# Holding the first superblock's transposing load until W0 has landed

## The chip, the cores and the metric

The kernel runs on one core of a Trainium2 chip. The metric is the device time of one execution in microseconds (us), lower is better. It is measured by repeated executions; beside it stands one execution recorded by the hardware profiler, from which all durations below are taken.

## The reference

A deep-and-cross network with six layers over a batch of 4096 rows with 416 features, all bf16:

```python
B, F, D, L = 4096, 26, 16, 6
Din = min(F * D, 1024)          # 416
def reference(x0, ws, bs):      # x0 [4096,416], ws [6,416,416], bs [6,416]
    x = x0
    for l in range(ws.shape[0]):
        x = x0 * (x @ ws[l] + bs[l]) + x
    return x
```

The kernel carries it as a sum of matrix products that stays in PSUM: each layer adds its product to the running sum, and one VectorE operation per tile adds a bias and multiplies by x0 to make the next layer's input.

## The kernel before

**Tiling.** The batch is cut into NS = 4 superblocks of SB = 1024 rows, and each goes through the L = 6 layers. The 416 features are three blocks of 128 (index c or k, NC = 3) and a tail of 32. Activations are held transposed, with features on partitions: x0T_sb is x0 for the three blocks, x0t_sb the tail. Each superblock has two halves of H = 512 columns. `n = s * L + l` counts the layer steps.

**One layer step on TensorE**, in program order: (1) nine groups of four matmuls, 512 columns each, for half 0 (lines 347 to 363); (2) the tail rows, ten matmuls with 32 rows (lines 388 to 409), which end by adding one to `s_ti`; (3) the tail's own output, twelve matmuls of 256 columns over all 1024 columns (lines 413 to 419); (4) nine groups of four for half 1 (line 420). TensorE runs its instructions in order, so a wait in front of (3) holds everything behind it. VectorE makes the six 128x512 tiles of the next layer (line 527): three for half 0 after (2), three for half 1 as (4) brings them.

**Where the first superblock gets x0T.** Rows 0 to 767 are loaded in natural layout as three 208 KB pieces (`xin_sb`, lines 135 to 137), transposed on TensorE and copied out by VectorE and ScalarE. Rows 768 to 1023 come by a single DMA that transposes on its way, line 157: 256 rows by 384 columns of two bytes, 192 KB. Its semaphore is `s_x0T[0]`. The only instruction that waits for it is TensorE's at line 412, between (2) and (3) of step n = 0, since (3) is the first to read columns 768 to 1023.

**Who issues what at the start.** Before the block: SP issues the biases, `xin_sb` rows 0 to 255 and rows 512 to 767; ScalarE's queue issues `xin_sb` rows 256 to 511, then W0 (`s_w[0]`, 312 KB), then `xtl_sb` (the tail of rows 768 to 1023), then two tail-weight loads; GpSimd issues six small weight loads. In the block SP issues in this order: the transposing load of line 157; W1 (line 163); four tail-weight loads for layers 1 to 5 (line 166, made at line 125, `s_wt[1]`); W2, after the wait at line 160 for `s_ti` to reach 1; and so on. SP runs in order too: a wait on SP stands in front of all of this.

**Who waits for W0.** TensorE at line 346, in front of its first matmul with weights. That matmul also waits, at line 339, for the third VectorE copy of x0T.

**Who waits for the rest of SP's list.** Line 360 waits for W1 ahead of step n = 1, line 378 for `s_wt[1]` ahead of that step's tail rows.

Of the kernel before, what the change touches and what calls it, by code (L numbers as in the profile page):

```python
# [11 lines left out]
def bass_standalone__dcn_v2_cross__recsys_kernel(  # L12
# [20 lines left out]
    with ExitStack() as es:  # L33
# [30 lines left out]
        def sem(name):  # L64
            return es.enter_context(nc.semaphore(name))
# [6 lines left out]
        s_w = [sem("s_w%d" % i) for i in range(L)]  # L72
# [18 lines left out]
        def wmain(l):  # L91
            return ws[l, 0:DF, :].rearrange("(k p) n -> p k n", p=128)
# [12 lines left out]
        def lane(g):  # L105
            return slice(32 * g, 32 * g + 32)
# [9 lines left out]
        def store(eng, a, n, by_pool):  # L116
            eng.wait_ge(s_o, a + n - by_pool)
            if by_pool:
                eng.wait_ge(s_oP, by_pool)
            assert a % 2 == 0 and n == 2  # L120
            eng.dma_start(out_w[:, (j0 + a) // 2, :, :], o_sb[:, j0 + a:j0 + a + n, :]).then_inc(s_out, 16)

        def load_wt(eng, g, a, b, done):
            n0, n1 = ((0, 256), (256, DF))[g % 2]
            eng.dma_start(
                wt_sb[lane(g), a:b, 0:n1 - n0], ws[a:b, DF:D, n0:n1].rearrange("l p n -> p l n")
            ).then_inc(done, 16)
# [19 lines left out]
        @block.sync  # L147
        def _(sp):
            def load_rows(s):
                sp.dma_start_transpose(  # L150
                    x4_sb[:, s - 1:s, :], x0[s * SB:(s + 1) * SB, D - 128:D]
                ).then_inc(s_x4[s - 1], 16)
                sp.dma_start_transpose(
                    x0T_sb[:, :, s * SB:(s + 1) * SB], x0[s * SB:(s + 1) * SB, 0:DF]
                ).then_inc(s_x0T[s], 16)

            sp.dma_start_transpose(x0T_sb[:, :, 768:SB], x0[768:SB, 0:DF]).then_inc(s_x0T[0], 16)
            for l in range(1, L):
                if l > 1:
                    sp.wait_ge(s_ti, (1, 2, 2, 2)[l - 2])  # L160
                if l == L - 1:
                    load_rows(1)
                sp.dma_start(w_sb[:, l, :, :], wmain(l)).then_inc(s_w[l], 16)
                if l == 1:
                    for g in range(4):
                        load_wt(sp, g, 1, L, s_wt[1])
            for s in range(NS - 1):
                n = (s + 1) * L
                sp.wait_ge(s_xa, NC * n)
                sp.wait_ge(s_xb, NC * n)  # L170
                for c in range(NC):
                    sp.dma_start_transpose(
                        o_sb[:, s * JS:(s + 1) * JS, c * 128:(c + 1) * 128], xo_sb[:, s, c, :]
                    ).then_inc(s_oT, 16)
                sp.wait_ge(s_xt, n)
                sp.dma_start_transpose(ot_sb[:, s, :, :], xot_sb[:, s, :]).then_inc(s_ot, 16)
                if s < NS - 2:
                    load_rows(s + 2)
                if s == 0:
                    for g in range(4):  # L180
                        sp.dma_start(wl_sb[lane(g), :], ws[L - 1, DF:D, :]).then_inc(s_wl, 16)
                if s == 1:
                    sp.dma_start(x0n_sb[:, :, :].rearrange("p (g r) d -> p g r d", r=2), x0_w[:, j0 // 2:, :, :]).then_inc(s_x0n, 16)
                sp.wait_ge(s_oT, 16 * NC * (s + 1))
                sp.wait_ge(s_otc, s + 1)
                sp.dma_start(
                    out_v[:, s * JS:(s + 1) * JS, :], o_sb[:, s * JS:(s + 1) * JS, :]
                ).then_inc(s_out, 16)
            store(sp, 0, 2, 0)
            store(sp, 4, 2, 2)  # L190
# [458 lines left out]
```

## Time and profile before

| what | value |
|---|---|
| median of 4 runs | 128.25 us (128.12 to 128.37) |
| the profiled execution, its own time | 128.29 us |
| its span in the profile | 127.0 us |
| TensorE clock granted, every slice | 1.0 in nearly every stretch (9 tenths or more in all 40 slices) |
| DVE busy | 99.9 us (79%) |
| ACT busy | 67.6 us (53%) |
| POOL busy | 24.0 us (19%) |
| mean DMA traffic | 106 GB/s |

The span runs from the first to the last recorded instruction; 1.3 us of the execution's own time lie outside it. PE is TensorE's matmul side and PEld its weight loads, which overlap the matmuls; DVE is VectorE, ACT ScalarE, POOL GpSimd, and a q behind an engine's name means its sequencer, which issues DMAs. Busy shares are averages over the span. Matmul ends are modelled, so a busy PE does not mean that no matmul could have started earlier; where TensorE waited is better read from the starts of its weight loads. Besides the page, the trace holds a start and a size for each DMA packet and the time of each landing (the increment of a semaphore by one of the 16 DMA engines); where a time below has three decimals, it is from these records.

### The profile page before, as it was taken

The page shows a single profiled execution, that of the slowest core. Times are in us where ns is not written, and L with a number is a line of the kernel's source. Part 1 is how long each engine was busy: PE and PEld are TensorE (multiplying, and loading weights), DVE is VectorE, ACT ScalarE, POOL GpSimd, SP SyncE. Part 2 cuts the span into 40 slices and gives each one's busy share as a digit, 9 for nine tenths or more (in the row PEclk, how much of TensorE's full clock was granted, in tenths as well). Part 3 has the DMA queues.
Part 4 walks back from the last instruction along what each step waited for, and adds up shares of the span by engine and source line. Part 5 has one row for each costly group of instructions (what it writes and reads, how often), then busy time and mean ns, then how long its engine had stood idle before and what let it go on. Part 6 is the DMA issues. An engine that isn't in the chain of part 4 may idle for free.

```text
span 127.0 us, 5318 instructions
## 1 busy us (share of the span) xinstructions
PE 123.5 (97%) x2410; PEld 62.4 (49%) x2410; DVE 99.9 (79%) x154; ACT 67.6 (53%) x146; POOL 24.0 (19%) x44
## 2 busy tenths in 40 slices
PE   7999999999999999999999999999999999999991
PEld 5654544444445445445445445445444444454660
DVE  2449779779779779789788797797797797797973
ACT  0637357377726455575744563575762574566830
POOL 7512202102102013022022023022021021220450
PEclk9999999999999999999999999999999999999999
DMA  3963299400009969810007779940005900430006
GB/s 108 316 154 106 81 270 181 110 0 0 5 3 113 168 108 238 260 32 5 5 0 137 137 131 240 355 151 0 5 0 48 210 21 0 164 109 5 0 30 243
DMA packets 32577, 13.49 MB, mean 106 GB/s; under 512 B 24870, under 2 KB 32556, under 8 KB 32556
## 3 DMA queue, kind: packets, MB, share of 16 engines
q1 hardware_dynamic: 31036, 12.12, 43.7%
q10 hardware_dynamic: 1328, 0.99, 2.5%
q8 instruction: 19, 0.31, 1.0%
q0 software_dynamic: 192, 0.06, 0.2%
q14 instruction: 2, 0.02, 0.0%
HBM read 3.86 MB, written 3.41 MB: 57 GB/s over the span
## 4 chain that ended last, share of the span: by engine, by line
PE 97%; DVE 0%; issue 0%
PE ps L255 82%; PE ps L383 10%; PE ps L130 2%; PE ps L439 2%; PE ps L302 1%; PE ps L454 1%; DVE o_sb L540 0%; PE ps L478 0%; PE ps L399 0%; PE ps L484 0%
## 5 line engine op out<-in xcount | busy, mean ns | idle before, releaser
L527 DVE SCALAR_TENSOR_TENSOR xT_sb<-ps,cb_sb,x0T_sb 128x512 bf16<-128x512 f32 x120 | 81.0, 745 | 16.3 <-PE ps L383 16.3
L255 PE MATMUL ps<-xT_sb,w_sb 128*32 128x512 bf16 (+1 forms) x1596 | 84.2, 364 | 0.0
L255 PEld LDWEIGHTS ps<-xT_sb,w_sb 128*32 128x32 bf16 x1596 | 40.9, 97 | 37.2 <-issue 4.0
L556 ACT ACTIVATE xt_sb<-xt_sb 32x256 bf16<-32x256 bf16 x76 | 31.5, 414 | 15.7 <-POOL xt_sb L232 15.1
L585 ACT ACTIVATE t_sb<-ps,cb_sb 64x256 f32<-64x256 f32 x46 | 21.6, 469 | 31.1 <-PE ps L255 30.8
L232 POOL TENSOR_TENSOR xt_sb<-t_sb,x0t_sb 128x256 bf16<-128x256 f32 x20 | 13.4, 672 | 81.4 <-ACT t_sb L585 81.4
L255 PE MATMUL ps<-x0T_sb,w_sb 128*32 128x512 bf16 (+1 forms) x336 | 18.7, 367 | 0.0
L527 DVE SCALAR_TENSOR_TENSOR xo_sb<-ps,cb_sb,x0T_sb 128x512 bf16<-128x512 f32 x18 | 12.1, 744 | 2.5 <-PE ps L383 2.5
L255 PEld LDWEIGHTS ps<-x0T_sb,w_sb 128*32 128x32 bf16 x336 | 8.6, 97 | 7.8 <-issue 1.1
L383 PE MATMUL ps<-xt_sb,wt_sb 32*128 32x512 bf16 x76 | 11.5, 379 | 0.0
L604 ACT ACTIVATE x0t_sb<-x_sb 32x512 bf16<-32x512 bf16 x12 | 7.5, 626 | 0.3
L399 PE MATMUL ps<-xt_sb,wt_sb 32*128 32x512 bf16 x38 | 7.4, 385 | 0.0
L383 PE MATMUL ps<-xt_sb,wc_sb 32*128 32x256 bf16 x76 | 7.3, 268 | 0.0
L383 PEld LDWEIGHTS ps<-xt_sb,wt_sb 32*128 32x128 bf16 x76 | 2.2, 92 | 8.1 <-DVE xT_sb L527 8.1
L383 PEld LDWEIGHTS ps<-xt_sb,wc_sb 32*128 32x128 bf16 x76 | 3.8, 93 | 2.2
L232 POOL TENSOR_TENSOR xot_sb<-t_sb,x0t_sb 128x256 bf16<-128x256 f32 x3 | 2.0, 673 | 12.6 <-ACT t_sb L585 12.6
L540 DVE SCALAR_TENSOR_TENSOR o_sb<-ps,x0n_sb 128x416 bf16<-128x416 f32 x6 | 3.3, 586 | 1.0 <-PE ps L484 0.9
L560 ACT ACTIVATE xo_sb<-ps,cq_sb 128x512 bf16<-128x512 f32 x5 | 3.3, 685 | 1.1 <-PE ps L383 1.1
L551 ACT ACT_TABLE_LOAD x1 | 1.3, 1283 | 3.6 <-issue 3.6
L130 PE MATMUL ps<-const-bfloat16-1.0 128*32 128x256 bf16 x40 | 2.3, 418 | 0.8 <-PEq L634 0.8
L439 PE MATMUL ps<-w_sb,xT_sb 128*128 128x416 bf16 x12 | 2.8, 340 | 0.0
L255 PE MATMUL ps<-w_sb,xT_sb 128*32 128x416 bf16 x48 | 2.6, 339 | 0.0
(52 smaller groups left out, 39.8 us busy)
## 6 DMA issues: line engine op xcount, KB each, us to landing
out_dram<-o_sb SPq DMA_DIRECT2D x3, 832.0 KB, 4.5
w_sb<-in_ws_dram SPq DMA_DIRECT2D x5, 312.0 KB, 3.7
x0n_sb<-in_x_dram SPq DMA_DIRECT2D x1, 832.0 KB, 5.5
xin_sb<-in_x_dram SPq DMA_DIRECT2D x2, 208.0 KB, 3.5
out_dram<-o_sb SPq DMA_DIRECT2D x2, 208.0 KB, 1.9
out_dram<-o_sb ACTq DMA_DIRECT2D x2, 208.0 KB, 2.0
w_sb<-in_ws_dram ACTq DMA_DIRECT2D x1, 312.0 KB, 3.7
xin_sb<-in_x_dram ACTq DMA_DIRECT2D x1, 208.0 KB, 2.6
```

The source lines that it names most:

```text
L130: nc.tensor.matmul(ps[lane(q % 4), 7, 0:256], lhsT=CONST[:, 0:32], rhs=CONST, start=True, stop=True, skip_group_check=True, tile_position= ...
L232: pool.tensor_tensor(out=dst, in0=t32_sb[:, n % 2, :], in1=x0t_sb[:, s, 0:G], op=ALU.mult).then_inc(s_xt, 1)
L255: return pe.matmul(dst, lhsT=lhsT, rhs=rhs, start=start, stop=True, skip_group_check=True, tile_position=(0, 32 * q),)
L383: return pe.matmul(dst, lhsT=lhsT, rhs=srct[lane(g), cols], start=l == 0 and start, stop=True, skip_group_check=True, tile_position=(32 * ...
L399: pe.matmul(ps[:, NC * h + 2, :], lhsT=wt_sb[lane(g), l, 0:128], rhs=srct[lane(g), :].rearrange("p (b r) -> p b r", b=2)[:, ::-1, :], star ...
L439: pe.matmul(ps[:, NAT_BANKS[t], 0:D], lhsT=xT_sb[:, (L - 1) % 2, k, rows], rhs=w_sb[:, L - 1, k, :], start=False, stop=True, skip_group_ch ...
L527: dve.scalar_tensor_tensor(out=dst, in0=ps[:, NC * half + c, :], scalar=cb_sb[:, c, l:l + 1], in1=x0T_sb[:, c, o:o + H], op0=ALU.add, op1= ...
L540: dve.scalar_tensor_tensor(out=o_sb[:, j0 + t, :], in0=ps[:, NAT_BANKS[t], 0:D], scalar=1.0, in1=x0n_sb[:, t, :], op0=ALU.add, op1=ALU.mul ...
L556: ins = act.activation(out=buf[lane(g), G:2 * G], in_=buf[lane(g ^ 1), 0:G], func=ACTF.Copy)
L560: act.activation(out=xo_sb[:, NS - 1, c, half * H:(half + 1) * H], in_=ps[:, NC * half + c, :], func=ACTF.Identity, bias=cq_sb[:, c:c + 1] ...
L585: ins = act.activation(out=t32_sb[HALVES[h], n % 2, :], in_=tail(h), func=ACTF.Identity, bias=cb_sb[HALVES[h], NC, l:l + 1],)
L604: ins = act.activation(out=x0t_sb[lane(g), s + 1, :].rearrange("p (b n) -> p b n", b=2), in_=src[:, ::-1, :] if g % 2 else src, func=ACTF. ...
```

## The change

One wait is added on SP in front of the transposing load of line 157. It waits until W0's semaphore has its full count of 16. Nothing else differs: the load, its semaphore, its reader and the order of SP's list are the same.

```diff
                     x0T_sb[:, :, s * SB:(s + 1) * SB], x0[s * SB:(s + 1) * SB, 0:DF]
                 ).then_inc(s_x0T[s], 16)
 
+            sp.wait_ge(s_w[0], 16)
             sp.dma_start_transpose(x0T_sb[:, :, 768:SB], x0[768:SB, 0:DF]).then_inc(s_x0T[0], 16)
             for l in range(1, L):
                 if l > 1:
```

## The prediction

> **What bounds the kernel.** I read the page first: the busy shares and the chain of work that ended last.
>
> ```profile
> PE 123.5 (97%) x2410; PEld 62.4 (49%) x2410; DVE 99.9 (79%) x154; ACT 67.6 (53%) x146; POOL 24.0 (19%) x44
> ...
> PE 97%; DVE 0%; issue 0%
> ```
>
> TensorE carries the whole chain. Then the table of waits, for TensorE's weight-load side, where its waiting shows (total us, times, longest):
>
> ```profile
> PEld ps L383 <- DVE xT_sb L527: 8.1, 19, 0.4
> ...
> PEld ps L255 <- DMA w_sb<-in_ws_dram: 0.3, 1, 0.3
> ```
>
> Only one DMA ever makes TensorE wait: W0, 0.3 us, once. Now SP's own list and TensorE's weight loads, both in order of time (start, length, what):
>
> ```profile
> 2.22 1.28 SPq L157 DMA_TRANSPOSE x0T_sb<-in_x_dram  x1
> 3.55 0.58 SPq L163 DMA_DIRECT2D w_sb<-in_ws_dram  x1
> 4.17 1.92 SPq L125 DMA_DIRECT2D wt_sb<-in_ws_dram  x4
> 8.74 5.80 SPq L163 DMA_DIRECT2D w_sb<-in_ws_dram  x3
> ```
>
> ```profile
> 8.29 0.11 PEld L383 LDWEIGHTS ps<-x0t_sb,wc_sb 32*128 32x128 bf16 x3
> 8.61 1.96 PEld L255 LDWEIGHTS ps<-x0T_sb,w_sb 128*32 128x32 bf16 x48 [0.21 <-issue]
> 10.68 1.83 PEld L255 LDWEIGHTS ps<-xT_sb,w_sb 128*32 128x32 bf16 x36
> 12.94 0.09 PEld L383 LDWEIGHTS ps<-xt_sb,wt_sb 32*128 32x128 bf16 x1 [0.42 <-DVE xT_sb L527]
> ```
>
> The line at 8.61 is the first reader of the moved load (the matmuls behind line 412). Its 0.21 us of idle is "issue", so it did not wait for the load. The load was issued at 2.22 and took 5.0 us to land, so at 7.24. How late may it be? W0's last landing was 5.014 and the first weight load behind it started at 5.11: 0.10 us from landing to weight load. So the **deadline** is 8.61 - 0.10 = 8.51, and the slack today 8.51 - 7.24 = 1.27 us.
>
> **The change, step by step.**
>
> *SP's wait.* W0's last landing is 5.014. SP answers fast (its W2 issue at 8.736 came 0.02 us after the `s_ti` signal at 8.719), so the load is issued at **5.03** and not 2.22: 2.81 us later, against 1.27 us of slack. If the 5.0 us from issue to landing held, it would land at 10.03 and cost 1.5 us. It will not: in the packet records its 768 packets of 256 bytes start at 4.957, 2.73 us after the issue, because the same queue still carried `xin_sb` until about 5.0. After the change that queue is empty.
>
> *From issue to landing on an empty queue.* The nearest row is the other transposing load from DRAM, 1024 packets (line 150), issued at 43.57. Traffic by stretch (last two columns: DMA share, GB/s):
>
> ```profile
> 44.50:44.75 0.25, 0.25 (x12) 0.11 (x4) 0.25 (x1) 0.00 (x0) 0.25 (x1) 1.00 0.00 0
> 44.75:45.00 0.25, 0.25 (x10) 0.11 (x5) 0.25 (x2) 0.00 (x0) 0.23 (x1) 1.00 0.29 16
> ...
> 46.00:46.50 0.50, 0.50 (x16) 0.21 (x8) 0.50 (x2) 0.49 (x2) 0.00 (x0) 1.00 0.96 205
> 46.50:47.00 0.50, 0.50 (x12) 0.11 (x4) 0.40 (x1) 0.20 (x1) 0.00 (x0) 1.00 0.03 6
> ```
>
> Nothing moves until 44.75; the first packet is at 44.932, 1.36 us after the issue. From the first packet on I use the moved load itself: 4.957 to the landing at 7.238 is 2.28 us (1.2 us of packets, 1.1 us until the last landing, with W1's packets close behind it on the queue, as they will be again). Sum: 5.03 + 1.36 + 2.28 = **8.67**, which is 0.16 us past the deadline. The ends: the fastest transpose on an empty queue (line 172, issued at 66.457, on-chip source) landed after 3.2 us, so 8.23 and no wait; the line 150 loads on an empty queue took 3.4 and 3.5 us with a third more packets; the slow line 176 ones 3.8 and 3.9 us, so 8.93 and 0.42 us. I take 8.67, as it is made from the load's own packets.
>
> Here a rule speaks. The Trainium skill, "Advanced Engine Details and Errata", section "X-Bar Transpose (TRN2)", holds transposing DMAs to be as fast as regular ones. The regular row is W2, 312 KB on an empty queue at 8.74: it landed in 2.95 us. By the rule 192 KB would be there by 5.03 + 2.95 = 7.98, and the change would cost nothing. The transposing rows need 3.4 us for 256 KB where the plain one needs 2.95 for 312 KB, so I go with them.
>
> *What a wait there costs.* The wait stands in front of TensorE's parts (3) and (4). From 8.61 matmul groups follow each other every 0.216 us until 12.84; at 12.94 the tail rows start, just behind VectorE's last tile (its signal is at 12.890). VectorE's half-0 tiles hang on `s_ti`, which is given before the wait, so up to about a microsecond of the stall leaves VectorE as it is. But TensorE at 12.94 had waited only 0.1 us past its last group, and the turn from row to column tiles at 13.49 takes that long too without a wait. So 0 to 0.1 us can be absorbed; I take 0. Every later step is as tight, so the wait goes into the end in full: **0.16 us**.
>
> *What is queued behind SP's wait.* W1 moves from 3.55 to 5.03 + 1.28 + 0.05 = 6.36. W1 to W5 took 3.0 to 4.5 us to land: 9.3 to 10.9, wanted at 10.58 (10.68 less 0.10), which moves with any wait. The queue ahead of it holds only the moved load, so I take 3.7 us, 10.06: no wait; the upper end gives about 0.3 us, less the wait already taken. The four tail-weight loads move to 6.97 through 8.9, the last issued at about 8.46; the four landed 3.8 to 4.4 us after issue: 12.3 to 12.9, wanted at 12.71, when TensorE's wait for the swapped tail (signal at 12.679) ends. As their 4 us held the same standing queue, I take no wait; upper end 0.2 us. W2 is held by `s_ti` at 8.72 anyway and moves to about 8.9; with 2.95 us it is there by 11.9, wanted after 15.4.
>
> *What leaves the stretch from 4.9 to 6.2.* The packets of the moved load shared it with `xtl_sb` and the small weight loads. These may land sooner. TensorE's matmul groups run without a break through line 354 (6.626, 6.842), so `xtl_sb` gives nothing. The next weight load at 7.98 follows a VectorE cast (7.844) and a ScalarE copy (7.922), not a DMA; unbroken matmuls could have started at 7.85 in place of 8.01, so **0.16 us bounds any gain here**. W0 itself gains nothing: it had stopped sending packets by 4.75, before the moved load's first, and the third VectorE copy of x0T arrives at 5.003 against W0's 5.014.
>
> Sum: 128.29 + 0.16 = 128.45 us; the runs' median is 0.04 us below this execution's own time, well inside their spread.
>
> **The rivals.**
>
> *A: a short wait, 0 to 0.5 us (the sum above), 128.3 to 128.8.*
>
> *B: an instruction refill hits the load; slower.* The trace has an instruction fetch of 16 KB on one DMA engine that starts at 8.125 and takes 1.195 us. Refills that fell on transposes held them up. The one at 38.37, on the transpose issued at 37.25:
>
> ```profile
> 38.50:39.00 0.50, 0.50 (x16) 0.22 (x10) 0.50 (x2) 0.49 (x2) 0.00 (x0) 1.00 1.62 203
> 39.00:39.50 0.50, 0.50 (x17) 0.24 (x12) 0.50 (x2) 0.36 (x1) 0.00 (x0) 1.00 3.45 41
> 39.50:40.00 0.50, 0.50 (x16) 0.28 (x12) 0.50 (x2) 0.00 (x0) 0.49 (x1) 1.00 0.05 5
> ...
> 40.50:41.00 0.50, 0.50 (x20) 0.23 (x12) 0.50 (x2) 0.49 (x2) 0.00 (x0) 1.00 1.15 253
> ```
>
> Its traffic nearly stops for 1.5 us, and it lands 4.4 us after issue against 3.2 without. The tail transposes of line 176 met refills at 43.94 and 72.17: fifteen landings came by 44.62 and 72.86, the sixteenth at 46.17 and 74.31, 1.5 us later. Here the last packet should leave at 5.03 + 1.36 + 1.2 = 7.6, half a microsecond before the refill. From 8.1 on B decides: if anything of the load is then still outstanding on that engine, 0.6 (the smallest such delay, the transpose issued at 95.69) to 1.5 us come on top of 8.67. PE waits 0.8 to 1.7 us: 129.1 to 130.0. Against it the Trainium skill, "Runtime: NRT & Kernel Launch", section "Instruction fetch mechanics", calls a refill mostly hidden; by that B is worth nothing. For the engine whose program is fetched that may hold; for a transpose in flight these rows say 0.6 to 1.5 us.
>
> *C: W1 or the tail weights become late,* 0.2 to 0.8 us: 128.5 to 129.1. For it: landings of up to 4.5 us in the rows; against it: those stood in a full queue.
>
> *D: faster.* Needs the 0.16 us above to be won whole and no wait: 128.13, and that is still inside what can be told from no change. More is not to be found in the trace.
>
> That the wait doesn't bind is excluded: SP reaches it at 2.2, and W0 lands at 5.014.
>
> **How the numbers follow.** A measurement of this kernel tells 0.2% (0.26 us) from no change. A has 0.50: 0.38 within 0.26 us and 0.12 above. B 0.34, since half a microsecond of margin is small beside the 0.7 us over which the transposing rows spread. C 0.09. D, beyond 0.2%, 0.05, and the last 0.02 goes to no change. Faster 0.05, same 0.40, slower 0.55. The likeliest case gives 128.45, its own range 128.2 to 128.8. The range for 8 in 10 starts at 128.15, the runs' spread below no change, and goes to 129.8, all but B's last part.
>
> **What would show it.** The load issued at about 5.03 and landed at 8.2 to 8.9; the weight load of line 255 that stood at 8.61 now at 8.6 to 8.9, its idle time put down to the DMA of x0T_sb if it waited; the rest of the span moved by just that. B shows as one of the load's landings over 0.6 us behind the others, with the refill beside it. I am wrong if the load lands after 8.9 with no refill near it, if W1's landing ends a wait, or if the span gets shorter.

## The result, and the profile after

The changed kernel is slower by 0.52% (ratio to the kernel before 1.0052, 95% interval 1.0038 to 1.0065), which is 0.67 us of 128.5 us (0.49 to 0.84). The median of its 44 runs is 129.29 us; that of the 71 runs of the kernel before, taken beside it, is 128.52 us. The ratios here compare means that leave out runs more than 1.5% above the fastest of their kernel (five of the 71 and five of the 44), and the others still scatter much more than the first four did: 128.03 to 129.18 us for the kernel before, 128.26 to 130.12 us for the changed one. The profiled execution of the changed kernel lies near the lower end: 128.50 us of its own, a span of 127.3 us against 127.0.

Its page, the busy shares and the chain that ended last:

```profile
PE 123.6 (97%) x2410; PEld 62.3 (49%) x2410; DVE 100.0 (79%) x154; ACT 67.7 (53%) x146; POOL 24.1 (19%) x44
...
PE 89%; DMA 7%; SPq 1%; DVE 0%; ACTq 0%; issue 0%
PE ps L256 77%; PE ps L384 9%; DMA w_sb<-in_ws_dram 7%; PE ps L440 2%; SPq L158 1%; PE ps L455 1%; DVE o_sb L541 0%; PE ps L479 0%; ACTq L137 0%; PE ps L400 0%; PE ps L485 0%
```

The busy shares tell nothing. The chain does: 7% of it is now a load of weights, and 1% is SP's queue at line 158, the moved load (every line is one further down than before). But the chain reaches back through everything that the last link waited for; where TensorE stood is in its waits and its weight loads, which follow, with SP's list, all of the changed kernel (first TensorE's waits for weights: us in total, times, longest):

```profile
PEld ps L256 <- DMA w_sb<-in_ws_dram: 0.8, 2, 0.6
```

```profile
5.17 1.29 SPq L158 DMA_TRANSPOSE x0T_sb<-in_x_dram  x1
6.50 0.58 SPq L164 DMA_DIRECT2D w_sb<-in_ws_dram  x1
7.13 3.49 SPq L125 DMA_DIRECT2D wt_sb<-in_ws_dram  x4
10.66 4.54 SPq L164 DMA_DIRECT2D w_sb<-in_ws_dram  x3
```

```profile
8.58 1.96 PEld L256 LDWEIGHTS ps<-x0T_sb,w_sb 128*32 128x32 bf16 x48 [0.21 <-issue]
11.10 1.63 PEld L256 LDWEIGHTS ps<-xT_sb,w_sb 128*32 128x32 bf16 x36 [0.56 <-DMA w_sb<-in_ws_dram]
13.16 0.09 PEld L384 LDWEIGHTS ps<-xt_sb,wt_sb 32*128 32x128 bf16 x1 [0.42 <-DVE xT_sb L528]
```

The moved load is there in time: its reader starts at 8.58, with the same 0.21 us of "issue" as before. Two waits for weights are left, W0's of before and a new one of 0.56 us at 11.10: **W1**, the load behind the moved one on SP. SP's four tail-weight loads took 3.49 us to issue, not 1.92. The tail rows of layer 1 start at 13.16 in place of 12.94, and the 0.22 us between these is, to 0.01 us, the whole difference of the spans. In all fourteen profiles of this study, from the first matmul of these tail rows to the start of the last instruction it is 114.08 to 114.10 us: **everything that differs happens ahead of them, in the first 13 to 14 us of these two kernels.**

Why was W1 late? By the packet records W1's sixteen landings were 9.159 to 9.985 for fifteen and **11.057** for the last. A 16 KB instruction refill started at 7.729, with W1's first packet (7.733), and kept one DMA engine for 1.784 us, until 9.513. All but 24 of W1's 384 packets had started by 9.457; those 24, one sixteenth of the load, start one after another from 9.509 to 10.546. So one engine's share of W1 stood behind the refill. A last landing that comes far behind the fifteenth is called a straggler below. That gives two theories for the runs: W, W1 is what arrives late, with the refill as its cause; T, the moved transposing load is what is usually late, and this one profile missed it.

### The profile page after: what moved, and what is told of

Its sections match the earlier page's. It is cut to its first block, busy times and chain, and to the rows that moved or that the text cites. A ratio compares the mean times of both kernels' runs of the same rounds, so it can differ in the third digit from the quotient of the medians.

```text
span 127.3 us, 5318 instructions
## 1 busy us (share of the span) xinstructions
PE 123.6 (97%) x2410; PEld 62.3 (49%) x2410; DVE 100.0 (79%) x154; ACT 67.7 (53%) x146; POOL 24.1 (19%) x44
## 4 chain that ended last, share of the span: by engine, by line
PE 89%; DMA 7%; SPq 1%; DVE 0%; ACTq 0%; issue 0%
PE ps L256 77%; PE ps L384 9%; DMA w_sb<-in_ws_dram 7%; PE ps L440 2%; SPq L158 1%; PE ps L455 1%; DVE o_sb L541 0%; PE ps L479 0%; ACTq L137 0%; PE ps L400 0%; PE ps L485 0%
```

## The experiments

**The changed kernel again, twice.** No edit.

> The changed kernel once more, for its spread and a second profile. Theory W (W1 is what arrives late, because an instruction refill holds one of its 16 landings): 0.4 to 0.8% slower than before, and the profile shows TensorE's weight load of layer 1 waiting for the DMA of W1, 0.5 us or more. Theory T (the moved transposing load is late in most executions, and the first profile happened to miss that): the same time, but here the weight load that stood at 8.6 us waits for the DMA of x0T_sb.

> The changed kernel for a third time, on the same chip as the two above. Theory W: 0.3 to 0.6% slower than before, and a third profile with TensorE waiting for W1, whose last landing comes 1 us or more behind the fifteenth. If the first two profiles were chance and the typical loss is another, the wait stands elsewhere, ahead of line 412's matmuls or at W0.

Measured: 1.0025 (1.0003 to 1.0047), less than theory W asked, and 1.0058 (1.0036 to 1.0081). TensorE's weight loads in the second and third profile:

```profile
8.52 1.96 PEld L256 LDWEIGHTS ps<-x0T_sb,w_sb 128*32 128x32 bf16 x48 [0.21 <-issue]
11.56 1.63 PEld L256 LDWEIGHTS ps<-xT_sb,w_sb 128*32 128x32 bf16 x36 [1.08 <-DMA w_sb<-in_ws_dram]
```

```profile
9.45 1.96 PEld L256 LDWEIGHTS ps<-x0T_sb,w_sb 128*32 128x32 bf16 x48 [0.21 <-issue]
11.99 1.63 PEld L256 LDWEIGHTS ps<-xT_sb,w_sb 128*32 128x32 bf16 x36 [0.58 <-DMA w_sb<-in_ws_dram]
```

Three profiles of three wait for W1 and none for the moved load, which landed at 8.14, 8.17 and 8.02. Theory T falls. The third is also late at 9.45; that is another matter, at the end. A clean measure of the wait: where nothing waits, it is 2.28 us from the first matmul behind line 413 to the first of layer 1 (in all nine profiles without a wait for W1, the kernel before among them: 8.615 to 10.895). Here it is 2.52, 3.04 and 2.54 us, so W1 costs **0.24, 0.76 and 0.26 us**.

**Only W1 and the tail weights late.** The kernel before with one wait, behind the transposing load:

```diff
             sp.dma_start_transpose(x0T_sb[:, :, 768:SB], x0[768:SB, 0:DF]).then_inc(s_x0T[0], 16)
+            sp.wait_ge(s_xtl0, 16)
```

> The transposing load is back at its old place without a wait; only what follows it on SP (W1 and the tail weights) is held, until the load of xtl_sb has landed, about 6.5 us, where the changed kernel issues W1. Theory W: as slow as the changed kernel, 0.4 to 0.8% over before, with TensorE waiting for W1. Theory T: no slower than before, within 0.2%.

Measured: 1.0009 (0.9986 to 1.0031). The time is unclear: it leaves room for no change and for a part of the loss, not for what theory W asked. The trace is plain: W1 issued at 6.618, fifteen landings by 9.839, the last at 11.408, and

```profile
11.45 1.63 PEld L256 LDWEIGHTS ps<-xT_sb,w_sb 128*32 128x32 bf16 x36 [0.70 <-DMA w_sb<-in_ws_dram]
```

that is 2.66 us where 2.28 is free: 0.38 us, with the transposing load at its old place. So the wait for W1 does not need the late load.

**Only the load and the tail weights late.** W1 ahead of the wait:

```diff
+            sp.dma_start(w_sb[:, 1, :, :], wmain(1)).then_inc(s_w[1], 16)
             sp.wait_ge(s_w[0], 16)
             sp.dma_start_transpose(x0T_sb[:, :, 768:SB], x0[768:SB, 0:DF]).then_inc(s_x0T[0], 16)
             for l in range(1, L):
...
-                sp.dma_start(w_sb[:, l, :, :], wmain(l)).then_inc(s_w[l], 16)
+                if l > 1:
+                    sp.dma_start(w_sb[:, l, :, :], wmain(l)).then_inc(s_w[l], 16)
```

> W1 is issued first, then the wait for W0, then the transposing load, then the tail weights: only the load and the tail weights are late. Theory W: within 0.2% of before. Theory T: 0.4 to 0.8% slower, with a wait for x0T_sb ahead of line 412's matmuls. If the late tail weights are the cause, it is slower too, but with the wait at the tail rows of layer 1, near 12.9 us.

Measured: 1.0018 (0.9999 to 1.0038), on the edge of no change. W1 landed at 7.46 and nobody waits for it (2.28 us), but now the load is late:

```profile
8.92 1.96 PEld L258 LDWEIGHTS ps<-x0T_sb,w_sb 128*32 128x32 bf16 x48 [0.42 <-DMA x0T_sb<-in_x_dram]
10.99 1.83 PEld L258 LDWEIGHTS ps<-xT_sb,w_sb 128*32 128x32 bf16 x36
```

It was issued at 4.985 and landed at 8.878, 3.9 us later and not 3.0; its last packet left at 7.902, behind the refill's start at 7.687 (in the changed kernel's profiles the last one left at 7.55 to 7.68). All sixteen landings are late here, from 8.363 on, so it is not W1's pattern; whether the refill held the load or W1's packets, which still shared the queue until 6.615, is not shown.

**The refill moved, four kernels.** The first refill comes when some 300 of TensorE's recorded instructions have started (304 before, 296 changed), so it should move with their number. The kernel starts with warm-up matmuls on constants, before any load is there. Cutting them finer brings it earlier, making them larger later; they do about the same array columns. (The count turned out to be rough: with other warm-ups the refill came after 240 to 279.) Earlier, 128 instructions more, in the changed kernel and in the kernel before:

```diff
-        for q in range(4 * 10):
+        for q in range(4 * 26):
             nc.tensor.matmul(
-                ps[lane(q % 4), 7, 0:256], lhsT=CONST[:, 0:32], rhs=CONST, start=True, stop=True,
+                ps[lane(q % 4), 7, 0:100], lhsT=CONST[:, 0:32], rhs=CONST[:, 0:100], start=True, stop=True,
```

> The changed kernel with its warm-up matmuls cut finer: 104 of 100 columns in place of 40 of 256, about the same TensorE time and 128 more instructions, so that the instruction refill that started at 7.7 us comes some 128 instructions earlier, at 5 to 6 us, when SP's queue is empty here. Theory W with the refill as its cause: W1 lands some 3 us after its issue and without a straggler, TensorE does not wait for it, and the kernel is within 0.2% of before. If W1 is late without the refill too (a plain queueing delay): 0.4 to 0.8% slower, as the changed kernel.

> The kernel before with the same finer warm-up matmuls, as the control. The refill then falls on the packets of the transposing load, between 4.9 and 6.2 us. Under the theory that a refill holds back what shares its DMA engine, the load lands later than 7.2 us, at 8.2 to 8.8, and the time is between no change and 0.3% slower. If refills do not matter: within 0.1% of before.

Measured: the changed kernel 1.0017 (0.9990 to 1.0044). The refill came at 5.320. W1 landed without a straggler (fifteenth 10.944, last 10.980, 3.7 us after its issue), and TensorE took 2.28 us: no wait for it. But the refill met W0: fifteenth landing 4.939, last 5.960. TensorE waits for it, and its next six groups of matmuls come only every 0.43 us (the last section), so that this profile spans 129.4 us:

```profile
6.00 0.14 PEld L256 LDWEIGHTS ps<-x0T_sb,w_sb 128*32 128x32 bf16 x8 [1.15 <-DMA w_sb<-in_ws_dram]
```

So taking the refill off W1 gained nothing that can be told: in this execution it cost the start instead, and the median of all 22 runs is 129.29 us against 128.70.

The kernel before: **1.0102** (1.0077 to 1.0128), far more than I expected. The refill came at 5.150 and met, besides the transposing load (landed 8.66), the x0 piece of rows 512 to 767 and `xtl_sb`, which landed at 7.17 and 7.52 (5.71 and 6.48 in the first profile of before):

```profile
7.62 0.14 PEld L255 LDWEIGHTS ps<-ident,xin_sb 128*32 128x32 bf16 x4 [1.28 <-DMA xin_sb<-in_x_dram]
```

Nothing of the DMA list was touched here. 128 instructions more on TensorE cost 1% through a wait for loads, and I had looked at one load only. Ten of the sixteen landings of the x0 piece are late here (6.90 and after), not one; how a refill holds so many is not shown.

Later, 76 instructions fewer (in both kernels; the four 256-column matmuls of `fill` became one of 128x128 as well):

```diff
-        for q in range(4 * 10):
+        CONST5 = nc.const_aps.tensor_like(1.0, x4_sb[:, 0, 0:512])
+        for q in range(5):
             nc.tensor.matmul(
-                ps[lane(q % 4), 7, 0:256], lhsT=CONST[:, 0:32], rhs=CONST, start=True, stop=True,
-                skip_group_check=True, tile_position=(0, 32 * (q % 4)),
+                ps[:, 7, 0:512], lhsT=CONST5[:, 0:128], rhs=CONST5, start=True, stop=True, skip_group_check=True,
             )
```

> The changed kernel with its warm-up made of fewer, larger matmuls: 5 of 128x128 by 512 columns in place of 40 of 128x32 by 256, and 1 in place of 4 at the second place. TensorE's array passes the same columns, with 76 instructions fewer, so that the refill that started at 7.7 us comes some 76 instructions later, near 9.6 us, when W1 has left the queue. Theory W with the refill as its cause: W1's last landing is by 10.2 us, at most 3.7 us after its issue; TensorE doesn't wait for it; the time is within 0.2% of before. If W1 is late without the refill: TensorE waits for it again and the time stays 0.3 to 0.6% over before. The refill may now fall on the tail weights instead, which have until 12.7 us.

> The control: the kernel before with the same larger warm-up matmuls. Both theories: within 0.2% of before. It also shows whether the larger warm-up does anything by itself.

Measured: changed kernel 1.0033 (1.0012 to 1.0053), kernel before 1.0013 (0.9992 to 1.0033). The experiment missed its aim: the refill moved to 8.641 only, still among W1's packets (7.531 to 9.451 without the straggler's), and W1 was late again, fifteenth 10.119, last 11.431, 0.72 us of wait. It shows only that where the refill still meets W1, the straggler is still there.

**A shorter hold.** The wait for W0 replaced by one for an x0 piece:

```diff
-            sp.wait_ge(s_w[0], 16)
+            sp.wait_ge(s_xin[1], 16)
```

> SP waits for the x0 piece that lands at about 4.3 us (rows 0 to 255) and not for W0 at 5.0 us: the load is issued near 4.3 us and W1 near 5.6 us, so the hold is 2.1 us and not 2.9. Theory W: W1's packets leave before the refill or just as it starts; W1 lands by about 9 us, with a straggler by 10.4 us at the latest, where it is wanted at 10.85 us: no wait for W1, and the time within 0.2% of before. If any hold costs in proportion to its length: 0.3 to 0.5% slower.

Measured: 1.0004 (0.9985 to 1.0023): no loss. The hold is shorter than I wrote, since this semaphore counts the piece of rows 256 to 511, which is the first to land: the load went out at 3.540 and W1 at 4.870, so it is 1.3 us. W1's packets ended at 8.556, the refill started at 8.742; fifteenth landing 9.456, last 9.463; 2.28 us to layer 1. This profile has another wait, for `xtl_sb` (landed 7.331). A hold that leaves W1 clear of the refill showed no loss, then.

**The refill in the empty stretch.** The changed kernel with 100 warm-up matmuls of 102 columns:

```diff
-        for q in range(4 * 10):
+        for q in range(4 * 25):
...
-                ps[lane(q % 4), 7, 0:256], lhsT=CONST[:, 0:32], rhs=CONST, start=True, stop=True,
+                ps[lane(q % 4), 7, 0:102], lhsT=CONST[:, 0:32], rhs=CONST[:, 0:102], start=True, stop=True,
```

> The changed kernel with 100 warm-up matmuls of 102 columns, 120 instructions more, to put the refill at 5.3 to 6.4 us, where SP's queue is empty and W0 has landed. Theory W: W1's last landing is within 0.3 us of its fifteenth and at most 3.8 us after its issue; TensorE does not wait for W1; 0 to 0.3% over before, less than the changed kernel's 0.5%. If the refill still meets W0's last landings, TensorE's start is late, and that alone sets the loss.

Measured: 1.0078 (1.0048 to 1.0108), from ten runs, 128.48 to 130.27 us: a miss, since theory W allowed 0.3%. The profile is the shortest of the ten and does what theory W asked: refill at 5.223, W1's fifteenth landing 10.360 and last 10.381, 2.28 us,

```profile
8.61 1.96 PEld L256 LDWEIGHTS ps<-x0T_sb,w_sb 128*32 128x32 bf16 x48 [0.21 <-DMA x0T_sb<-in_x_dram]
10.68 1.83 PEld L256 LDWEIGHTS ps<-xT_sb,w_sb 128*32 128x32 bf16 x36
```

no wait for W1 (the 0.21 us put down to the moved load, landed at 8.415, stand there as "issue" too), only 0.1 us at layer 1's tail rows, for tail weights that landed at 12.907 (a second refill started at 10.260), and a span of 127.2 us. Why the other nine are up to 1.8 us longer this profile can't show. A refill that still meets W0's last landings, as in the kernel with 128 more, would do it; that is not shown. So the loss was not undone in either kernel that freed W1.

**The kernel before against itself.** No edit.

> The kernel before against itself, for the spread of this measurement and a second profile of it. All theories: ratio 1.000 within its interval; W1 lands near 8 us with its sixteenth landing within 0.3 us of its fifteenth; no wait for W1.

Measured: 1.0010 (0.9992 to 1.0028). W1's fifteenth landing 8.948, last 8.981; no wait for it. But this execution (128.97 us) has a wait that the first profile of the same kernel lacks:

```profile
7.25 0.14 PEld L255 LDWEIGHTS ps<-ident,xin_sb 128*32 128x32 bf16 x4 [0.77 <-DMA xin_sb<-in_x_dram]
...
9.30 1.96 PEld L255 LDWEIGHTS ps<-x0T_sb,w_sb 128*32 128x32 bf16 x48 [0.21 <-issue]
11.37 1.83 PEld L255 LDWEIGHTS ps<-xT_sb,w_sb 128*32 128x32 bf16 x36
```

The last to land ahead of these matmuls is `xtl_sb`, at 7.14, where the first profile had 6.48. It is queued on ScalarE behind W0 and shares its stretch with the transposing load, whose packets here took until 7.09 and not 6.16. In the changed kernel's three profiles that stretch is free and `xtl_sb` landed at 6.08, 6.08 and 5.96. So the change also takes something away: a wait that the kernel before has in some executions.

**That wait alone.** The kernel before, with `xtl_sb` issued by SP ahead of the x0 piece:

```diff
+        nc.sync.dma_start(xtl_sb[:, :, :], x0_v[:, 6:JS, DF:D]).then_inc(s_xtl0, 16)
         nc.sync.dma_start(xin_sb[:, 4:6, :], x0_v[:, 4:6, :]).then_inc(s_xin[2], 16)
...
-        nc.scalar.dma_start(xtl_sb[:, :, :], x0_v[:, 6:JS, DF:D]).then_inc(s_xtl0, 16)
```

> Not the change but what its runs point to. In the second profile of the kernel before, TensorE waits at line 354 for the small load of xtl_sb, which lands at 7.1 us because the transposing load and the small weight loads share its stretch; with the change it lands at 6.0 to 6.1 us in every profile. Here there is no wait on SP; the load of xtl_sb alone moves, from the end of ScalarE's queue to SP's, ahead of the x0 piece of rows 512 to 767. If that wait is a part of the kernel before's usual time: xtl_sb lands before 5 us, no wait for it, W1 lands near 8 to 9 us, 0.1 to 0.4% faster than before. If the second profile was an exception: within 0.1% of before. If the moved load now delays the x0 piece past 6.6 us, TensorE waits for that instead: no gain.

Measured: 0.9998 (0.9973 to 1.0024), no gain. `xtl_sb` landed at 5.96, but the x0 piece at 6.95 (5.71 in the first profile of before) and W0 at 5.41, and TensorE waits for both. I found no version that beats the kernel before.

**All profiles side by side**, from the packet records (us). The last column is the time beyond 2.28 from line 413's matmuls to layer 1:

| kernel | W1's packets, first and last | refill starts | W1 landings: 15th, last | wait for W1 |
|---|---|---|---|---|
| before, its two profiles | 5.960 to 7.052; 6.869 to 7.966 | 8.125; 8.973 | 7.824, 8.004; 8.948, 8.981 | 0; 0 |
| before, refill earlier / later | 7.234 to 8.451; 6.051 to 7.196 | 5.150; 8.272 | 9.287, 9.294; 7.980, 8.160 | 0; 0 |
| shorter hold | 6.536 to 8.556 | 8.742 | 9.456, 9.463 | 0 |
| W1 first | 5.035 to 6.615 | 7.687 | 7.231, 7.461 | 0 |
| xtl_sb early | 6.352 to 7.597 | 8.297 | 8.413, 8.504 | 0 |
| changed, refill earlier, two kernels | 8.543 to 10.340; 7.895 to 9.698 | 5.320; 5.223 | 10.944, 10.980; 10.360, 10.381 | 0; 0 |
| changed, three profiles | 7.733, 7.679, 7.581, to 10.546, 11.004, 11.293 | 7.729; 7.668; 8.491 | 9.985, 11.057; 10.090, 11.515; 10.012, 11.944 | 0.24; 0.76; 0.26 |
| changed, refill later | 7.531 to 10.922 | 8.641 | 10.119, 11.431 | 0.72 |
| W1 alone late | 7.661 to 10.891 | 7.785 | 9.839, 11.408 | 0.38 |

In the five profiles where a refill started with or among W1's packets, the last landing is 1.07 to 1.93 us behind the fifteenth; in the nine others 0.01 to 0.23. Every wait for W1 is among the five. In each of the five the last packets of W1 (24 of 384; 13 with the refill later) start one after another from the refill's end on: from 9.509, 9.731, 10.031, 10.059 and 9.629, where the refill ends at 9.513, 9.744, 10.045, 10.073 and 9.644 (three of the changed kernel, refill later, W1 alone late). So one engine's share stood until the refill was done, and the fifteen others did not. (In the third profile of the changed kernel that engine had started none of W1 by 8.491, when the refill is first seen, 0.9 us behind the others; what held it until then is not known.) (One profile of each kind was seen before the theory was formed; the other twelve came after.)

## Why the prediction was right, and where it was wrong

The forecast was 128.45 us in a range of 128.15 to 129.8, with slower as the likeliest sign. The sign and the range held; the path was another. The summed wait of 0.16 us, at the moved load, was in none of the three profiles, and the wait that they do show is for W1, which the sum put at nothing. So it is luck that the sign held. By the prediction's own sign, "if W1's landing ends a wait", it was wrong in its mechanism.

*SP's wait.* Held: the load went out at 5.168, 5.105 and 5.023 for a predicted 5.03, always 0.02 us after W0's last landing.

*From issue to landing.* **This step failed**, the term of 2.28 us from the first packet to the landing. I put the landing at 8.67 and a wait of 0.16 us; it was 8.14, 8.17 and 8.02, ahead of the 8.51 deadline, and the wait was nothing. The first 1.36 us were right (first packet 1.36, 1.36 and 1.37 after issue); the rest took 1.62, 1.71 and 1.64 us. I had taken the 2.28 from the old place, where the load shared its stretch with other queues and W1 came close behind. Here its packets took 1.1 to 1.2 us, as there, but the landing followed 0.5 us after the last and not 1.1. W1 behind it is not the reason: with W1 alone late, the load at its old place landed 1.3 us after its last packet (6.573, 7.889). That leaves the x0 piece ahead of it and the other queues, which is not shown. The bound of 3.2 us from the fastest transpose was the better row, and even that was 0.1 to 0.2 too long. The slow end of 3.8 and 3.9 us was misread: those two tail transposes are the ones that refills had met, and the third of line 176 landed in 2.39 us. Against the rule of the Trainium skill, "Advanced Engine Details and Errata", section "X-Bar Transpose (TRN2)", that I set aside: the load landed after 2.97, 3.07 and 3.00 us for 192 KB, where W2 with its 312 KB had 2.95. For the time it gives, no stall at the load, the rule would have been the better guide here; in speed per byte it still does not hold.

*What is queued behind SP's wait.* **This step failed too, and it is the one that cost a wait.** I let W1 land at 10.06 and took no wait. Fifteen of its sixteen landings were there by 9.99, 10.09 and 10.01: the estimate was good and the wrong thing to estimate, because TensorE waits for all sixteen, and the last came at 11.06, 11.52 and 11.94. The deadline was mis-sized too, the other way: I took the weight load at 10.68, but that one waits in front of its matmul at 10.895, and W1's last landing led its matmul by 0.04 us (11.057, 11.101), so W1 had until about 10.85. This is rival C, with 0.24 to 0.76 us within its 0.2 to 0.8, though for a cause that I had given to rival B. I gave it 0.09.

*Rival B.* The mechanism was right, 1.1 to 1.9 us on one engine's landing for an estimate of 0.6 to 1.5; the victim was wrong. What I had set against it did not hold: this refill was not hidden, and TensorE stood 0.24 to 0.76 us for the load that it held. I had asked where the refill at 8.125 stands to the one load that the change names. The load was gone by then (last packet 7.55 to 7.68), and what the change had moved into the refill's way was the next one in the list.

*What leaves the stretch from 4.9 to 6.2.* I bounded the gain at 0.16 us from one profile in which `xtl_sb` came just in time. In the second one of the same kernel it came late, and TensorE waited. How often it does can't be told from its landings in two profiles of before and one with the larger warm-up (6.48, 7.14 and 6.27). What the change costs is, by the profiles, W1's wait less this one.

*What goes into the end.* I took a stall as going into the end in full, and it does: 114.08 to 114.10 us from layer 1's tail rows on, whatever came before.

**What stays open.** That the refill makes W1 late, and that TensorE then waits for W1, is shown. That this is the whole of the loss is not. The three waits for W1 average 0.42 us; the measured loss is 0.67 (0.49 to 0.84). Layer 1's tail rows start at 13.16, 13.61 and 14.04 in the changed kernel's profiles and at 12.94 and 13.63 in those of before. These means differ by 0.32 us, and the slow start of TensorE in the third profile alone (0.98 us, the last section) is that much; W1's waits are about made up for by the wait for `xtl_sb` in the second profile of before. Whether the change makes slow starts more frequent was not tried. Nor does every execution lose: the fastest of the changed kernel's second set took 127.99 us, beside 127.94 for the fastest of before. And the test that would close it failed: the two changed kernels that freed W1 put the refill near W0, and neither is shown to be back at the time of before.

## What to carry to other kernels

A wait in front of one DMA holds the whole list behind it: give each later transfer its own new landing time, deadline and neighbours, and take the last of its sixteen landings, not the bulk. Look for instruction refills in the trace where a load's slack is less than such a straggler (1.07 to 1.93 us here). In this kernel the first refill moved with the number of TensorE's instructions ahead of it (128 more brought it from 8.1 to 5.2 us), so that adding instructions cost 1% with no load touched. And take a second profile before a wait is called absent: the kernel before had one in its second profile that the first lacked.

## What was not expected of the hardware

*While a refill ran, an issue on SP stood.* In the changed kernel one tail-weight load of SP's list took 2.003, 2.543 and 1.981 us to issue in the three profiles (0.44 to 0.48 us in the first profile of before), and ended 0.1 to 0.4 us after the refill did; SP's next loads all went out that much later. The same stands in four other kernels' profiles (1.28 to 2.46 us), but a transposing load issued during a refill took its usual 1.28 us (changed kernel, refill earlier). Why it is so is not shown.

*TensorE's clock at the start.* In the third profile of the changed kernel the first matmul groups come every 0.43 us, and later every 0.216 (weight loads, four to a group):

```profile
5.57 0.18 PEld L256 LDWEIGHTS ps<-x0T_sb,w_sb 128*32 128x32 bf16 x4 [0.25 <-issue]
5.99 0.18 PEld L256 LDWEIGHTS ps<-x0T_sb,w_sb 128*32 128x32 bf16 x4 [0.25 <-issue]
6.42 0.18 PEld L256 LDWEIGHTS ps<-x0T_sb,w_sb 128*32 128x32 bf16 x4 [0.25 <-issue]
6.84 0.18 PEld L256 LDWEIGHTS ps<-x0T_sb,w_sb 128*32 128x32 bf16 x4 [0.25 <-issue]
```

Five such groups (0.38 to 0.43 us each) cost 0.98 us beyond 0.216 each, and they are why that profile stands at 9.45 where the others have 8.52 and 8.58. The first profile of before has one (0.381), the second profile of the changed kernel none. The granted clock in the profile's rows is 1.00 throughout, but the trace's clock records behind these rows begin only at 5.563 us in the first profile of before, within the second group, after which the groups come every 0.216; at 9.664 in the changed kernel with the refill earlier, whose groups come every 0.43 us until 8.967; and this third profile has none. Where nothing was recorded, the rows show 1.00. The Trainium skill, "TensorE: Matmul & The Clock Gate", Part 1, describes a clock that is halved until a free-running activity window has passed, so that the turn varies from run to run; its 426.7 and 215.7 ns for 512 columns are the rows' 0.427 and 0.216. This may be a part of the scatter of single runs, in both kernels; that was not tried.
